# Transposing K of batches 2 and 3 in two steps of two head pairs, where there were four of one

## The chip, the cores and the metric

The kernel runs on one core of a Trainium2 chip. The metric is the device time of one execution in microseconds (us), taken as the median of several runs. A profile is one further execution with every engine recorded. Engines: TensorE (PE; its weight loads are PEld), VectorE (DVE), ScalarE (ACT), GpSimd (POOL) and SyncE (SP, which here only issues DMAs).

## The reference

Eight batches, 8 heads, 576 positions, head dimension 64. Attention with a decay bias and a causal mask, then RMS norm and a SwiGLU feed-forward network over all 4608 tokens:

```python
scores = (1 / sqrt(D)) * q @ k.T                        # per batch and head, 576 x 576
cum    = cumsum(maximum(s, 0)); bias = -(cum_i - cum_j)
scores = where(causal, -1e9, scores + minimum(bias, 0))
x      = softmax(scores) @ v                            # heads side by side: 4608 x 512
xn     = x / sqrt(mean(x * x) + 1e-6) * rms_g
out    = (silu(xn @ w_gate) * (xn @ w_val)) @ w_out     # 512 -> 1536 -> 512
```

Inputs and output are float32; the kernel multiplies in bfloat16.

## The kernel before

**Two kinds of work on one PE.** After batch 0, which is done by a prologue written out by hand, the feed-forward network runs in nine chunks of 512 tokens, and the attention of batches 1 to 7 is woven into it. `ffn(c)` (L658) is the frame. For each of 12 blocks `fb` of the hidden dimension it issues four gate matmuls (G, L668), a Tanh on ACT (L671), four value matmuls (V, L677) and on DVE the two products U (L680) and Ht (L673). Then come four output tiles of 12 matmuls (O, L690), each copied out by ACT (L695) and stored by SP (L697). G, V and O use four PSUM buffers in turn (`psF`): G of block `fb+2` takes the buffer of G of block `fb`, which is free once U of block `fb` has read it.

**The planner.** Between these groups `ffn` calls `step()` (L599), 36 times a chunk. One call is a *slot*. Chunk c has slots 36c+1 to 36c+36; 24 of them lie in the G/V part and 12 in the O part. The order that results is fixed when the program is built; every engine then runs its own instructions in that order and waits on semaphores. Slots are counted, not timed: the rules ask how many slots ago something was issued. In a slot `step()` does, in this order: what the last S step left pending; at most one `x_scale` (L335, DVE) with its `xt_dma` (L342, a DMA transpose on SP's queue); one item of ACT's side queue (loads of K and Q); one DMA transpose of Q or K (`kq_dma`, L171, on SP's queue); one item of the V loads and of POOL's casts; one check on DVE (L369, L375); and then PE work: an S step alone, or else an AV step and a T step if both are allowed.

The steps of attention, for batch b, with `g` for the two halves of the heads (head pairs 0 and 1, or 2 and 3):

- **T** (`t_step`, L180): K of one head pair is transposed by four PE matmuls against the identity into the bank `psT`, and one ACT copy (L192) spreads the 512 columns into `kqT`. `tail_step` (L194) does the same for the last 64 positions of all head pairs. In batches 2 and 3 K goes this way and Q goes through `kq_dma`; from batch 4 (`KB`) on there is no T at all. `psT` has one buffer, and AV with g = 1 uses it too (`psT32`).
- **S** (`s_step`, L225): scores of key block kb (0 to 4) and half g, then the exponentials on ACT (L274), half of them in the slot after, and the causal mask on POOL (L283). `psS` has one buffer.
- **AV** (`av_step`, L292): attention times V, a reciprocal and a product on DVE (L313, L315); with g = 1 also a sum of squares on ACT (L321) and its inverse root on POOL (L328, L331).
- **XT**: `x_scale` three slots after AV(b, qb, 1), and `xt_dma`, which puts 128 tokens into `xnT`. G of chunk c reads all 512 tokens of the chunk from there.

**What sets the order.** `t_seq`, `s_seq` and `av_seq` are consumed in order. `can_t` (L530) wants, for b of 2 or more:

```python
if b >= XB and at(*(("XT", 1, 3) if b == 2 else ("AV", b - 1, (2, 1, 0, 0, 0)[b - 3], 1))) > slot[0]:
    return False
if b >= XB and av_seq[0][2] == 1 and can_av(True):
    return False
if slot[0] - last["T"] < (1 if b < XB else 2 if b < 4 else 3) or slot[0] - last["AVT"] < 3:
    return False
```

So T of batch 3 may begin once AV(2, 2, 1) is done, two T steps are two slots apart, and a T step is three slots away from an AV step with g = 1 (`last["AVT"]`), in both directions. `can_s` (L540) wants the T steps of its two head pairs three slots back, the Q transposes five slots back, a free slot among eight E buffers, and a distance to the last S step that depends on a due time:

```python
due = SLOTS * ((b * S + kb * 128) // DM) - (26 if b == 1 else 18 if b < 4 else 14)
if slot[0] - last["S"] < (4 if slot[0] < due - 24 else 3 if slot[0] < due else 2):
```

`can_av` (L561) wants its S steps five slots back, two slots since the last AV, and XT of four row blocks earlier. `done["T", b, hp, w]`, written by `do_t` (L489), is where S looks for its transposes; `after_tail` queues the loads and casts of batch b + 2.

Of the kernel before, what the change touches and what calls it, by code (L numbers as in the profile page):

```python
# [12 lines left out]
AF = mybir.ActivationFunctionType  # L13
# [13 lines left out]
def kernel(  # L27
# [12 lines left out]
    nc = tc.nc  # L40
# [9 lines left out]
    HP = H // 2  # L50
# [7 lines left out]
    ident_bf = pers.tile([128, 128], BF16, name="ident_bf")  # L58
# [18 lines left out]
    kqn = mp.tile([128, 2, 2, NSC, H, D], BF16, name="kqn")  # L77
# [3 lines left out]
    kqTn = kqT.rearrange("d a w (h n) -> d a w h n", h=HP)  # L81
    kqTx = kqT.rearrange("d a w (c h n) -> d a w c h n", c=NSC, h=HP)
    XB = 2
    KB = 4
# [19 lines left out]
    def psF16():  # L104
        return pp.tile([128, 8, 128], BF16, name="psF16", tag="F", bufs=4)
# [10 lines left out]
    def psT():  # L116
        return pp.tile([128, 8, 128], BF16, name="psT", tag="T", bufs=1)
# [62 lines left out]
    def t_step(b, hp, w, pT=None, dve=None):  # L180
        pT = psT() if pT is None else pT
        dve = (w == 1) if dve is None else dve
        for r in range(4):
            nc.tensor.matmul(
                pT[:, r, :], lhsT=kqn[:, b % 2, w, r, 2 * hp:2 * hp + 2, :],
                rhs=ident_bf, is_transpose=True, start=(r == 0), stop=(r == 3))
        dst = kqTn[:, b % 2, w, hp, 0:512].rearrange("d (p r) -> d p r", r=4)
        src = pT[:, 0:4, :].rearrange("d r p -> d p r")
        if dve:
            nc.vector.tensor_copy(out=dst, in_=src)  # L190
        else:
            nc.scalar.activation(out=dst, in_=src, func=AF.Copy)  # L192

    def tail_step(b):  # L194
        pT = psT()
        nw = 2 if b < XB else 1
        for w in range(nw):
            for hp in range(HP):
                i = w * HP + hp
                nc.tensor.matmul(  # L200
                    pT[:, i, :], lhsT=kqn[:, b % 2, w, 4, 2 * hp:2 * hp + 2, :],
                    rhs=ident_bf, is_transpose=True, start=(i == 0), stop=(i == nw * HP - 1))
        dst, src = kqTn[:, b % 2, 0, :, 512:576], pT[:, 0:HP, 0:64]
        if b == 0:
            nc.vector.tensor_copy(out=dst, in_=src)
        else:
            nc.scalar.activation(out=dst, in_=src, func=AF.Copy)
        if nw == 2:
            nc.vector.tensor_copy(out=kqTn[:, b % 2, 1, :, 512:576], in_=pT[:, HP:8, 0:64])
# [163 lines left out]
    def check_max(i):  # L373
# [7 lines left out]
    slot = [0]  # L381
    first, chunk = [0], [0]
    done = {}
# [2 lines left out]
    s_seq.sort(key=lambda x: (1, 0, x[2], x[1]) if x[0] == 1 and x[1] < 2 else (x[0], x[1], x[2], 0))  # L386
    av_seq = [(b, qb, g) for b in range(B) for qb in range(NSC) for g in (0, 1)]
    xt_seq = [(b, qb) for b in range(B) for qb in range(NSC)]
    t_seq = [(b, hp, w) for b in range(KB) for hp in list(range(HP)) + ["tail"]
             for w in (0, 1) if w == 0 or (hp != "tail" and b < XB)]  # L390
    t_seq.sort(key=lambda x: (x[0], 9, 0, 0) if x[1] == "tail" else
               (x[0], x[1] // 2, x[2], x[1]) if x[0] == 1 else (x[0], x[2], x[1], 0))
# [86 lines left out]
    def after_tail(b):  # L479
        if b + 2 < B:  # L480
            casts(b + 2)
# [7 lines left out]
    def do_t(key, **kw):  # L489
        b, hp, w = key  # L490
        if hp == "tail":
            tail_step(b)
            done["T", b] = slot[0]
            after_tail(b)
        else:
            if b == 1:
                kw["dve"] = w == 1 and hp > 1
                if hp % 2:
                    kw["pT"] = psF16()
            t_step(b, hp, w, **kw)  # L500
        done["T", b, hp, w] = slot[0]
        last["T"] = slot[0]

    def do_s(key, pair=None):
# [94 lines left out]
    def step(bare=False):  # L599
# [31 lines left out]
        if can_s():  # L631
            pending.append(do_s(s_seq.pop(0)))
            if t_seq and t_seq[0][0] == 1 and can_t():
                do_t(t_seq.pop(0))
            return
# [7 lines left out]
        if n < 2 and t_seq and can_t():  # L643
            do_t(t_seq.pop(0))
# [126 lines left out]
    with tc.manual_schedule():  # L771
# [44 lines left out]
        load_v(0, 2)  # L816
        load_w(moe_w_gate, wg_sb, 0)
        do_t((0, 0, 0), pT=psT(), dve=False)
        do_t((0, 1, 0), pT=psF16(), dve=False)
        decay_sums()  # L820
# [65 lines left out]
        def done_cast(w):  # L886
# [11 lines left out]
                                        in_=moe_w_out.rearrange("(fc p) d -> p fc d", p=128)),  # L898
# [200 lines left out]
```

## Time and profile before

| | |
|---|---|
| median of 3 runs | 375.94 us (375.75 to 376.08) |
| the profiled execution | 375.92 us, span 374.2 us, 1.7 us outside it |
| PE busy | 347.0 us, 93% of the span |
| DVE, ACT, POOL busy | 279.7, 239.8, 174.4 us |
| T transposes (L184), all batches | 96 matmuls |
| ACT copies of T (L192) | 17, about 0.6 us each |
| granted TensorE clock | 0.998 of full |

The first G of chunk 1 starts 76.35 us into the span, of chunk 2 at 115.53 us, of chunk 3 at 155.60 us, of chunk 4 at 194.19 us. Busy shares are averages over the prologue, the woven stages and the last chunks, where no attention is left; stages have to be looked at one by one. A matmul's recorded duration is its passage through the pipeline (379 ns for one of 512 columns); what it takes from PE is the distance to the next start (a group of four: 0.86 us).

### The profile page before, as it was taken

What the parts mean: (1) busy time and instruction counts of PE and PEld (TensorE: products, weight loads), DVE (VectorE), ACT (ScalarE), POOL (GpSimd) and SP (SyncE); (2) the same over time, 40 slices, a digit from 0 to 9 for tenths busy, and PEclk for the clock granted to TensorE, in tenths of its full rate; (3) what the DMA queues carried; (4) which work ended last, traced back from release to release, by engine and by line L of the source; (5) the groups of instructions that cost most, each with busy time, mean ns of one, the idle gap of its engine ahead of it and who ended that gap; (6) DMA issues with size and microseconds to landing.
All of it is one profiled execution on the core that took longest, in us unless ns stands there. A gap on an engine that the chain in (4) does not pass through costs nothing. (4 is left out here: it accounts for less than half of the span.)

```text
span 374.2 us, 6937 instructions
## 1 busy us (share of the span) xinstructions
PE 347.0 (93%) x2356; PEld 161.4 (43%) x2356; DVE 279.7 (75%) x525; ACT 239.8 (64%) x626; POOL 174.4 (47%) x277
## 2 busy tenths in 40 slices
PE   1867899899999999899999999999999999999993
PEld 1443444454444444344444444444444444444441
DVE  6758988589887878788889897785488548837830
ACT  3777787547877597786777776777677744323321
POOL 5865734974846575779756825522322310000000
PEclk9999999999999999999999999999999999999999
DMA  8999999899997599959999997992210230020012
GB/s 230 189 227 237 146 196 220 123 204 225 155 168 105 53 195 165 159 55 204 149 162 225 136 107 152 120 67 44 96 26 14 44 105 3 0 84 31 0 44 76
DMA packets 125626, 46.22 MB, mean 124 GB/s; under 512 B 104912, under 2 KB 120784, under 8 KB 125584
## 3 DMA queue, kind: packets, MB, share of 16 engines
q0 software_dynamic: 59920, 11.80, 42.7%
q1 hardware_dynamic: 53040, 24.33, 34.6%
q10 hardware_dynamic: 12624, 9.59, 10.5%
q8 instruction: 20, 0.33, 0.4%
q14 instruction: 22, 0.18, 0.2%
HBM read 38.16 MB, written 9.44 MB: 127 GB/s over the span
## 5 line engine op out<-in xcount | busy, mean ns | idle before, releaser
L274 ACT ACTIVATE E<-psS,biasK 128x256 bf16<-128x256 f32 (+3 forms) x352 | 114.9, 415 | 19.7 <-PE psS L250 18.1
L668 PE MATMUL psF<-xnT,wg_sb 128*128 128x512 bf16 x432 | 111.1, 379 | 2.4 <-DMA xnT<-xs_sb 1.3
L677 PE MATMUL psF<-xnT,wv_sb 128*128 128x512 bf16 x432 | 111.1, 379 | 0.1
L690 PE MATMUL psF<-wout_sb,Ht 128*128 128x512 bf16 x432 | 102.3, 379 | 0.0
L283 POOL TENSOR_SCALAR_AFFINE_SELECT E<-E 128x512 bf16<-128x512 bf16 x72 | 52.2, 725 | 93.7 <-ACT E L274 92.8
L671 ACT ACTIVATE T<-psF 128x512 f32<-128x512 f32 x108 | 64.3, 597 | 42.1 <-PE psF L668 38.7
L680 DVE SCALAR_TENSOR_TENSOR U<-T,psF 128x512 bf16<-128x512 f32 x108 | 73.6, 682 | 21.9 <-ACT T L671 21.8
L673 DVE TENSOR_TENSOR Ht<-U,psF 128x512 bf16<-128x512 bf16 x99 | 67.7, 684 | 7.5 <-PE psS L250 0.5
L668 PEld LDWEIGHTS <-wg_sb 128*128 128x128 bf16 x432 | 38.7, 98 | 46.9 <-issue 8.0
L677 PEld LDWEIGHTS <-wv_sb 128*128 128x128 bf16 x432 | 38.6, 98 | 42.8 <-issue 4.6
L690 PEld LDWEIGHTS <-Ht 128*128 128x128 bf16 x432 | 38.7, 98 | 42.1 <-issue 2.3
L338 DVE SCALAR_TENSOR_TENSOR xs_sb<-x_sb,al_all,g_row 128x512 bf16<-128x512 bf16 (+1 forms) x40 | 32.8, 822 | 16.1 <-POOL al_all L331 14.5
L695 ACT ACTIVATE osb<-psF 128x512 f32<-128x512 f32 x36 | 21.4, 595 | 33.7 <-PE psF L690 29.4
L321 ACT ACTIVATE xs_sb<-x_sb 128x512 bf16<-128x512 bf16 (+1 forms) x36 | 22.9, 639 | 22.3 <-DVE x_sb L315 22.2
L175 POOL DMA_DIRECT2D v_sb<-in_v_dram x40 | 35.3, 883 | 0.4 <-issue 0.3
L375 DVE TENSOR_TENSOR acc<-acc,mag 128x1280 bf16<-128x1280 bf16 x32 | 29.4, 936 | 0.4
L250 PE MATMUL psS<-kqT 64*128 64x256 bf16 (+2 forms) x304 | 26.8, 262 | 1.6 <-ACT E L274 1.5
L306 PEld LDWEIGHTS <-E 128*128 128x128 bf16 x320 | 22.3, 99 | 13.3 <-POOL E L283 3.4
L328 POOL TENSOR_SCALAR al_all<-ss_all 128x1 f32<-128x1 f32 (+1 forms) x40 | 11.1, 277 | 28.5 <-ACT xs_sb L321 23.0
L300 PEld LDWEIGHTS <-E 128*128 128x128 bf16 x256 | 20.6, 99 | 7.9 <-DVE x_sb L315 0.6
L331 POOL TENSOR_TENSOR al_all<-al_all,mhalf 128x1 f32<-128x1 f32 (+1 forms) x40 | 22.2, 556 | 3.3
L250 PEld LDWEIGHTS <-kqT 64*128 64x128 bf16 x320 | 10.4, 97 | 29.9 <-issue 28.6
(94 smaller groups left out, 278.8 us busy)
## 6 DMA issues: line engine op xcount, KB each, us to landing
out_dram<-osb SPq DMA_DIRECT2D x36, 256.0 KB, 2.3
kq<-in_q_dram ACTq DMA_DIRECT2D x6, 1024.0 KB, 9.5
v_sb<-in_v_dram POOLq DMA_DIRECT2D x32, 128.0 KB, 7.2
kq<-in_k_dram ACTq DMA_DIRECT2D x2, 1024.0 KB, 10.6
kqn<-in_k_dram POOLq DMA_DIRECT2D x16, 128.0 KB, 5.6
wg_sb<-in_moe_w_gate_dram POOLq DMA_DIRECT2D x2, 768.0 KB, 7.3
wv_sb<-in_moe_w_val_dram POOLq DMA_DIRECT2D x2, 768.0 KB, 10.3
wout_sb<-in_moe_w_out_dram POOLq DMA_DIRECT2D x1, 1536.0 KB, 14.1
```

Of the source, the lines that this page charges most:

```text
L175: nc.gpsimd.dma_start(out=v_sb[0:n, b % 2, c, :, 0:64], in_=v[b, :, c * 128:c * 128 + n, :].rearrange("h p d -> p h d"))
L250: nc.tensor.matmul(pair[par][:, j * W:j * W + M], lhsT=kT, rhs=qT, start=(j == 0), stop=(j == nj - 1))
L274: nc.scalar.activation(out=eo, in_=ei, func=AF.Exp, scale=0.125, bias=biasK[:, kb, bh:bh + 1])
L283: nc.gpsimd.affine_select(out=Ev[:, :, 0:nq], in_=Ev[:, :, 0:nq], pattern=[[0, nh], [1, nq]], compare_op=ALU.is_ge, fill=0.0, base=0, chan ...
L338: nc.vector.scalar_tensor_tensor(out=xs_sb[0:n, (b * NSC + qb) % NX, :], in0=x_sb[0:n, (b * NSC + qb) % NX, :], scalar=al_all[0:n, col:col ...
L375: nc.vector.tensor_tensor(out=acc[:, sl], in0=acc[:, sl], in1=mag[:, sl], op=ALU.max)
L668: nc.tensor.matmul(Gp, lhsT=wg_sb[:, cc, fs], rhs=xnT[:, cc, x0:x0 + DM], start=(cc == 0), stop=(cc == CC - 1))
L671: nc.scalar.activation(out=T, in_=Gp, func=AF.Tanh, scale=0.5)
L673: nc.vector.tensor_tensor(out=Ht[:, fb - 1, :], in0=pend[0], in1=pend[1], op=ALU.mult)
L677: nc.tensor.matmul(Vp, lhsT=wv_sb[:, cc, fs], rhs=xnT[:, cc, x0:x0 + DM], start=(cc == 0), stop=(cc == CC - 1))
L680: nc.vector.scalar_tensor_tensor(out=U, in0=T, scalar=1.0, in1=Gp, op0=ALU.add, op1=ALU.mult)
L690: nc.tensor.matmul(Op, lhsT=Ht[:, fb, tb * 128:(tb + 1) * 128], rhs=wout_sb[:, fb, :], start=(fb == 0), stop=(fb == FB - 1))
```

## The change

For batches 2 and 3 (`b >= XB`; T steps exist only for b < 4) a T step takes two head pairs: eight transposes, which fill the whole bank `psT`, and then two copies on the same engine as before. `t_seq` lists head pairs 0 and 2 only, and `do_t` notes both head pairs as done in the step's slot. Batches 0 and 1 are unchanged, and so is `tail_step`.

```diff
     def t_step(b, hp, w, pT=None, dve=None):
...
-        for r in range(4):
+        nh = 1 if b < XB else 2
+        for i in range(4 * nh):
+            j, r = hp + i // 4, i % 4
             nc.tensor.matmul(
-                pT[:, r, :], lhsT=kqn[:, b % 2, w, r, 2 * hp:2 * hp + 2, :],
-                rhs=ident_bf, is_transpose=True, start=(r == 0), stop=(r == 3))
-        dst = kqTn[:, b % 2, w, hp, 0:512].rearrange("d (p r) -> d p r", r=4)
-        src = pT[:, 0:4, :].rearrange("d r p -> d p r")
-        if dve:
-            nc.vector.tensor_copy(out=dst, in_=src)
-        else:
-            nc.scalar.activation(out=dst, in_=src, func=AF.Copy)
+                pT[:, i, :], lhsT=kqn[:, b % 2, w, r, 2 * j:2 * j + 2, :],
+                rhs=ident_bf, is_transpose=True, start=(i == 0), stop=(i == 4 * nh - 1))
+        for i in range(nh):
+            dst = kqTn[:, b % 2, w, hp + i, 0:512].rearrange("d (p r) -> d p r", r=4)
+            src = pT[:, 4 * i:4 * i + 4, :].rearrange("d r p -> d p r")
+            if dve:
+                nc.vector.tensor_copy(out=dst, in_=src)
+            else:
+                nc.scalar.activation(out=dst, in_=src, func=AF.Copy)
...
-    t_seq = [(b, hp, w) for b in range(KB) for hp in list(range(HP)) + ["tail"]
+    t_seq = [(b, hp, w) for b in range(KB) for hp in list(range(0, HP, 1 if b < XB else 2)) + ["tail"]
              for w in (0, 1) if w == 0 or (hp != "tail" and b < XB)]
...
         done["T", b, hp, w] = slot[0]
+        if b >= XB and hp != "tail":
+            done["T", b, hp + 1, w] = slot[0]
         last["T"] = slot[0]
```

## The prediction

> **What bounds the kernel now.** I read the page's first part, then the waits of PE in the stage that the change touches, then the timeline there. The page:
>
> ```profile
> PE 347.0 (93%) x2356; PEld 161.4 (43%) x2356; DVE 279.7 (75%) x525; ACT 239.8 (64%) x626; POOL 174.4 (47%) x277
> ```
>
> PE is the bound, and what it idles is mostly prologue. The waits of PE between 76 and 156 us, chunks 1 and 2, which hold all T steps of batches 2 and 3 (line, what it waited for, us in total, times, longest):
>
> ```profile
> PE psF L668 <- DMA xnT<-xs_sb: 1.3, 1, 1.3
> PE psF L668 <- DVE U L680: 0.4, 1, 0.4
> PE psS L250 <- ACT E L274: 0.2, 1, 0.2
> ```
>
> Three places, under 2 us. A T step in the timeline (start, length, engine, line):
>
> ```profile
> 80.05 1.03 PE L668 MATMUL psF<-xnT,wg_sb 128*128 128x512 bf16 x4
> ...
> 80.91 0.39 PE L184 MATMUL psT<-ident_bf,kqn 128*128 128x128 bf16 x4
> ...
> 81.14 1.03 PE L677 MATMUL psF<-xnT,wv_sb 128*128 128x512 bf16 x4
> 81.17 0.60 ACT L671 ACTIVATE T<-psF 128x512 f32<-128x512 f32 x1 [0.67 <-PE psF L668]
> ...
> 81.67 0.59 ACT L192 ACTIVATE kqT<-psT 128x512 bf16<-128x512 bf16 x1
> ```
>
> Starts matter: G takes 80.91 - 80.05 = 0.86 us, four transposes 0.23 us, and V follows with no gap. A T step has no overhead on PE beside its transposes. The start of chunk 3:
>
> ```profile
> 151.24 1.21 SPq L348 DMA_TRANSPOSE xnT<-xs_sb  x1
> ...
> 153.91 0.39 PE L250 MATMUL psS<-kqT 64*128 64x256 bf16 x4
> ...
> 155.60 1.02 PE L668 MATMUL psF<-xnT,wg_sb 128*128 128x512 bf16 x4 [1.30 <-DMA xnT<-xs_sb]
> ```
>
> An S step takes 0.32 us (the one at 132.69 is followed by V at 133.01), so G was due at 154.23 and began 1.37 us late: the transpose of XT(3, 2), sent by SP at 151.24, had not landed.
>
> **The transposes and copies themselves: nothing.** Per batch four steps of four (4 x 0.223 us from the starts) become two of eight: 0.89 us of PE both times. Four copies of 0.60 us stay four; ACT, 64% busy, now has two in a row, 1.2 us. They issue no DMA. The PE's sum is unchanged, so anything gained or lost comes through the order. Its cover: behind the copies on ACT stand the next Tanh and the S step's exponentials. The first step's copies (batch 2) would begin where the row at 81.67 begins and end near 82.9; the second step's transposes come about 83.1, and the next Tanh after them. If that cover fails, the second step waits for `psT`: 0 to 0.15 us; I take +0.05.
>
> **The order, by stepping through the planner's rules.** Before, the rules give T of batch 2 in slots 41, 43, 45, 47 and its tail in 49; T of batch 3 in 67, 70, 77, 83 and tail in 85. In batch 3 two of these were held back because an AV step with g = 1 lay in between. After: batch 2 in 41 and 43, tail 45; S(2,0,0) in 44 instead of 46, S(2,0,1) 47 instead of 50, then S in 50, 53, 55, 57, 61, 65, 68 where it was 53, 55, 57, 59, 63, 66, 69. AV(2,2,1) comes in 62 instead of 64, which opens T of batch 3: slot 66 (beside AV(2,3,0)) and slot 69, before AV(2,3,1) is ready; tail in 75, ten slots earlier. So S(3,0,1) falls from slot 86 to 74, and the S steps of batch 3 stand three slots apart (71, 74, 77, 80, 83, 86, then 90, 94, 98) where four were crammed into 89, 91, 93, 95. AV(3,2,1) goes from 100 to 93, and XT(3,2) from 103 to 96. Batch 4 then runs 5 or 6 slots earlier than before (its V loads also finish before slot 96 instead of carrying over), batches 5 to 7 four. Loads and casts of batch 5, queued behind the tail of batch 3, stay where they were: their first item waits for the check of slot 100. On SP's queue XT(3,2) moves ahead of four Q and K transposes of batch 4; on POOL the inverse roots and masks come among casts (79 to 84) and V loads (from 85) instead of behind them.
>
> **What that is worth.**
>
> Chunk 3 starts at slot 109. With XT(3,2) seven slots earlier, at about 1.1 us a slot, 7.6 us lie against a lateness of 1.37: gone, -1.37.
>
> Two small waits in batch 2 go: the tail's transposes waited for the copy of step 47 (due 88.39 + 0.86 = 89.25, began 89.36), and a G waited for a late U (due 83.94, began 84.06): -0.22. What is late next there is V or G itself, at PE's rate.
>
> S steps that waited for the exponentials of the one before (`psS` has one buffer): an S step costs 0.10 us of gap by itself, and those at 134.90, 137.30 and 139.85 had 0.05, 0.11 and 0.15 more, the one at 101.36 had 0.23. At three or four slots of distance they go: -0.54.
>
> The wait of 0.4 us for U in chunk 1. The rows:
>
> ```profile
> 90.35 2.27 DVE L375 TENSOR_TENSOR acc<-acc,mag 128x1280 bf16<-128x1280 bf16 x1
> 90.39 1.17 POOL L149 CAST kqn<-kq 128x512 bf16<-128x512 f32 x2
> ...
> 92.54 0.67 DVE L680 SCALAR_TENSOR_TENSOR U<-T,psF 128x512 bf16<-128x512 f32 x1
> ...
> 93.27 1.02 PE L668 MATMUL psF<-xnT,wg_sb 128*128 128x512 bf16 x4 [0.38 <-DVE U L680]
> ```
>
> A check of 0.82 us (median of 32) took 2.27 beside POOL's casts; U came late, and G began 0.54 us after it was due (91.87 + 0.86). Check and casts keep their slots; AV(2,0,0), 0.60 us of DVE, moves into the check's slot, ahead of that U. Between the wait gone (-0.54) and all 0.60 us added I take +0.30, nearer the upper end, since what made it stands still. The Trainium skill (SBUF — State Buffer, "Who interferes with whom") says that a VectorE instruction with two SBUF inputs contends with a GpSimd one that reads SBUF, and that the first to issue blocks the other throughout; L375 beside a cast is that case and the trace agrees, 2.27 against 0.82 us. By the rule alone the stall recurs in full, and the sum below would be 374.7; were 0.82 us the rule, it would be 373.6.
>
> The end of G/V in chunk 2 gets denser on DVE. Slots 87 to 96: five U and five Ht (0.682 and 0.684 us), five AV (0.175 + 0.423), three x_scale (0.822): 12.3 us. PE in the same slots: ten groups of 0.863, two S of 0.43, five AV of 0.24: 10.7 us. DVE falls 1.6 us behind. G two blocks later needs U, so about one block (1.7 us) may be lost without a wait; and the first O tile reads the last Ht with its 12th matmul, which in the profile started near 143.91 (first at 141.30), while that Ht was done at 142.45: 1.46 us of margin. I take +0.30; from none to 3.8 (below).
>
> Batches 4 to 7: their waits (0.64, 0.30 and 0.20 us in the starts at 193.9, 212.1 and 179.1) may go (-1.1), or others of such size come (+0.6). I take 0.
>
> Sum: -1.37 - 0.22 - 0.54 + 0.30 + 0.30 + 0.05 = -1.48. The profiled execution took 375.92 us (span 374.2 and 1.7 around it, which nothing here touches), 0.02 from the median: 374.4.
>
> **Rivals.** *DVE becomes the bound at the end of chunk 2* (slower). Place: slots 87 to 96. An x_scale there can stretch to its longest (1.29 against 0.75 us) and wait for the inverse root as long as the longest in chunks 1 and 2 (0.7 us), with U and Ht queued behind it and PE behind those: three of them add 3.7 us to the lag of 1.6. Of these 5.3 us all beyond 1.46 is paid, 3.8 us instead of 0.30: 377.9. It turns the result from a lag of 3.2 us on. For it: DVE was busy 26.4 of the 28.45 us from 76.35 on, in chunk 1. Against: there, at the same load, it cost PE 0.65 us in all. [...] Chance 0.14.
>
> *The wait at chunk 3 stays* (no change): XT(3,2) is issued earlier by the planner, but SP sends in order, and five transposes of batch 4 took it 7.5 us from 130.84 on; x_scale itself may also be late. Then -1.37 is missing: 375.8. Against: 13 slots, some 14 us, remain to land it. Chance 0.12.
>
> *The later waits go too*: -1.1 more, 373.3. For it: S is one slot further apart there. Chance 0.13.
>
> That the change doesn't do what it says I leave out: bank, copies and `done` entries are plain in the diff.
>
> **Numbers.** The forecast, 374.4, has the remaining 0.61; by its unknowns alone it lies between 373.7 and 375.1. The range reaches to the other cases, 373.1 to 377.0, leaving out most of the slow rival's upper half and a little below. About 0.2% (0.75 us) is what a measurement of this kernel can tell from no change. Faster than that: forecast and third rival, less a little, 0.73; same: the second, 0.13; slower 0.14.
>
> **What would show it.** In the profile after: no DMA among PE's waits after 100 us; T steps of 0.45 us, two per batch, the last two before chunk 2 begins; L192 still 17 times 0.6 us; no S to S distance of two slots in chunk 2; PE without idle around the first O tile of chunk 2. A DVE wait of PE over 1 us there, or the DMA wait still at a chunk's start, would make the forecast wrong.

## The result: 0.8% slower, and the profile after

The changed kernel took 379.04 us in the median of six runs, 376.01 for the kernel before beside it: a ratio of 1.0077, 95% interval 1.0063 to 1.009. The forecast was 374.4 us. The profiled execution took 378.57 us, span 377.4 us; its mean granted clock was 0.987, but five other executions with 0.996 to 0.999 took 378.8 to 379.1 us, so the clock is not the cause.

The slots are those that the prediction derived, for each T, S and AV step of batches 2 and 3. The merged step itself runs as forecast, too. Its timeline, in the changed kernel (lines have moved by 3 to 6: G is L674, V L683, U L686, Ht L679, O L696, S L254, exponentials L278, sums of squares L325, AV's product L319, x_scale L342, checks L373 and L379):

```profile
80.88 0.61 PE L187 MATMUL psT<-ident_bf,kqn 128*128 128x128 bf16 x8
...
81.33 1.03 PE L683 MATMUL psF<-xnT,wv_sb 128*128 128x512 bf16 x4
...
81.63 1.08 ACT L196 ACTIVATE kqT<-psT 128x512 bf16<-128x512 bf16 x2
...
83.05 0.61 PE L187 MATMUL psT<-ident_bf,kqn 128*128 128x128 bf16 x8
```

Eight transposes take 0.45 us from start to start, the two copies are done at 82.7, and the second step follows its G (82.19 + 0.86) without a wait. The waits of PE over 76 to 200 us, the same columns as before (line, what it waited for, us in total, times, longest); the first line is the kernel before, whose waits for the DMA and for U in this longer window are those shown above (1.3 and 0.4 us):

```profile
PE psS L250 <- ACT E L274: 0.7, 2, 0.6
```

and the kernel after:

```profile
PE psS L254 <- ACT E L278: 5.0, 5, 1.5
PE psF L674 <- DVE U L686: 0.4, 1, 0.4
PE psF L683 <- DVE Ht L679: 0.3, 1, 0.3
```

The DMA wait of 1.3 us is gone, as forecast. In its place five S steps wait, 5.0 us together, for ACT to finish the exponentials of the S step before, which hold the only `psS`. From the starts of the PE groups between 76 and 215 us, everything over its usual length adds up to 6.7 us (3.9 before); the first matmul of the verdict (L756, the kernel's closing test of its ranges, after all attention) begins 2.8 us later. So, within what two single executions can tell, the whole loss is in these waits. The longest of them, and how it came about, DVE first:

```profile
90.33 2.12 DVE L379 TENSOR_TENSOR acc<-acc,mag 128x1280 bf16<-128x1280 bf16 x1
92.37 0.17 DVE L317 RECIPROCAL rZ<-psAV 128x4 f32<-128x4 f32 x1
92.57 0.42 DVE L319 TENSOR_TENSOR x_sb<-psAV,rZ 128x256 bf16<-128x256 f32 x1
92.91 0.68 DVE L686 SCALAR_TENSOR_TENSOR U<-T,psF 128x512 bf16<-128x512 f32 x1
...
95.11 0.42 DVE L319 TENSOR_TENSOR x_sb<-psT,rZ 128x256 bf16<-128x256 f32 x1
```

then ACT and the S step on PE:

```profile
95.57 0.63 ACT L325 ACTIVATE xs_sb<-x_sb 128x512 bf16<-128x512 bf16 x1 [1.99 <-DVE x_sb L319]
96.10 0.19 ACT L325 ACTIVATION_READ_ACCUMULATOR xs_sb<-x_sb 128x1 f32 x1
96.19 0.58 ACT L677 ACTIVATE T<-psF 128x512 f32<-128x512 f32 x1
96.67 1.56 ACT L278 ACTIVATE E<-psS,biasK 128x256 bf16<-128x256 f32 x4
...
98.28 0.39 PE L254 MATMUL psS<-kqT 64*128 64x256 bf16 x4 [1.45 <-ACT E L278]
```

Read it from the top. In slot 49 a check that takes 0.82 us elsewhere took 2.12 us beside POOL's casts, and AV(2,0,0), now in the same slot, stands behind it. The check is 1.3 us longer than usual and the two instructions of that AV step add 0.6, so the next U is almost 2 us late, and the product of AV(2,0,1), slot 52, ends at 95.5. The sum of squares of that step is in ACT's queue ahead of everything that came later. ACT idles 1.99 us in front of it, with the exponentials of S(2,1,1), slot 53, queued behind although their scores were done at 95.0; then the sum of squares and a Tanh take 1.1 us more, and the exponentials start at 96.67. S(2,2,0), slot 55, needs that `psS`, and PE stands for 1.45 us. It is a chain through four queues: DVE late, ACT's head of line, `psS`, PE.

### The profile page after: what moved, and what is told of

The parts are those of the page before. It is cut to its first block, busy times and chain, and to the rows that moved or that the text cites. A ratio compares the mean times of both kernels' runs of the same rounds, so it can differ in the third digit from the quotient of the medians.

```text
span 377.4 us, 6953 instructions
## 1 busy us (share of the span) xinstructions
PE 346.5 (92%) x2356; PEld 161.1 (43%) x2356; DVE 282.1 (75%) x525; ACT 239.4 (63%) x626; POOL 172.5 (46%) x277
## 4 chain that ended last, share of the span: by engine, by line
PE 46%; DVE 6%; POOL 4%; issue 3%; ACT 2%; POOLq 0%; DVEq 0%; ACTq 0%
PE psF L683 14%; PE psF L674 14%; PE psF L696 14%; PE psS L254 2%; DVE acc L379 1%; POOL v_sb L175 1%; DVE mag L373 1%; POOL kqn L155 1%; DVE Ht L679 1%; DVE x_sb L319 1%; POOL al_all L335 1%; ACT E L278 1%; DVE xs_sb L342 1%; DVE U L686 1%; POOL E L287 1%
## 5 line engine op out<-in xcount | busy, mean ns | idle before, releaser
L278 ACT ACTIVATE E<-psS,biasK 128x256 bf16<-128x256 f32 (+3 forms) x352 | 116.4, 415 | 19.9 <-PE psS L254 17.5
L674 PE MATMUL psF<-xnT,wg_sb 128*128 128x512 bf16 x432 | 111.2, 380 | 1.2 <-ACT xnT L368 0.7
L683 PE MATMUL psF<-xnT,wv_sb 128*128 128x512 bf16 x432 | 111.0, 379 | 0.5 <-DVE Ht L679 0.5
L696 PE MATMUL psF<-wout_sb,Ht 128*128 128x512 bf16 x432 | 101.9, 380 | 0.0
L686 DVE SCALAR_TENSOR_TENSOR U<-T,psF 128x512 bf16<-128x512 f32 x108 | 73.7, 682 | 22.9 <-ACT T L677 22.9
L679 DVE TENSOR_TENSOR Ht<-U,psF 128x512 bf16<-128x512 bf16 x99 | 67.8, 685 | 8.7 <-PE psS L254 1.0
L674 PEld LDWEIGHTS <-wg_sb 128*128 128x128 bf16 x432 | 38.7, 98 | 46.8 <-issue 7.0
L696 PEld LDWEIGHTS <-Ht 128*128 128x128 bf16 x432 | 38.8, 98 | 43.3 <-issue 3.1
L683 PEld LDWEIGHTS <-wv_sb 128*128 128x128 bf16 x432 | 38.7, 98 | 42.1 <-issue 3.5
L342 DVE SCALAR_TENSOR_TENSOR xs_sb<-x_sb,al_all,g_row 128x512 bf16<-128x512 bf16 (+1 forms) x40 | 34.0, 853 | 14.9 <-POOL al_all L335 13.1
L325 ACT ACTIVATE xs_sb<-x_sb 128x512 bf16<-128x512 bf16 (+1 forms) x36 | 22.9, 640 | 30.2 <-DVE x_sb L319 30.1
L254 PE MATMUL psS<-kqT 64*128 64x256 bf16 (+2 forms) x304 | 26.6, 261 | 5.8 <-ACT E L278 5.8
L379 DVE TENSOR_TENSOR acc<-acc,mag 128x1280 bf16<-128x1280 bf16 x32 | 29.1, 935 | 0.2
L254 PEld LDWEIGHTS <-kqT 64*128 64x128 bf16 x320 | 10.4, 97 | 34.3 <-issue 33.8
L332 POOL TENSOR_SCALAR al_all<-ss_all 128x1 f32<-128x1 f32 (+1 forms) x40 | 9.6, 239 | 32.4 <-ACT xs_sb L325 26.4
```

The lines of the kernel that those rows point to most:

```text
L254: nc.tensor.matmul(pair[par][:, j * W:j * W + M], lhsT=kT, rhs=qT, start=(j == 0), stop=(j == nj - 1))
L278: nc.scalar.activation(out=eo, in_=ei, func=AF.Exp, scale=0.125, bias=biasK[:, kb, bh:bh + 1])
L342: nc.vector.scalar_tensor_tensor(out=xs_sb[0:n, (b * NSC + qb) % NX, :], in0=x_sb[0:n, (b * NSC + qb) % NX, :], scalar=al_all[0:n, col:col ...
L379: nc.vector.tensor_tensor(out=acc[:, sl], in0=acc[:, sl], in1=mag[:, sl], op=ALU.max)
L674: nc.tensor.matmul(Gp, lhsT=wg_sb[:, cc, fs], rhs=xnT[:, cc, x0:x0 + DM], start=(cc == 0), stop=(cc == CC - 1))
L679: nc.vector.tensor_tensor(out=Ht[:, fb - 1, :], in0=pend[0], in1=pend[1], op=ALU.mult)
```

## Experiments

Three theories. *A, later D:* the merge costs nothing; the new order puts an AV step with g = 1 in the slot ahead of an S step where DVE is late, and DVE's lateness reaches PE through the sum of squares, the exponentials and `psS`. *M:* the merged step itself costs, by two copies in a row. *L:* ACT is simply outrun by S steps three slots apart.

### 1. The merge alone, in the old order

```diff
+        if b >= XB:
+            return slot[0] == AT[b, hp]      # 43, 47, 49; 70, 83, 85
...
+        if slot[0] in (41, 45, 67, 77):
+            last["T"] = slot[0]
```

> The merged T steps, but every S, AV and XT step in the slot it had before the change (merged T in slots 43 and 47, 70 and 83; tails 49 and 85). Theory A (the loss is the order: an AV step with g = 1 now stands in the slot ahead of S steps, its sum of squares on ACT waits for DVE, and the exponentials behind it keep psS): the time is that of before, 375.5 to 376.5 us, and the PE waits for psS stay near the 0.2 us that the profile of before has between 76 and 156 us. Rival M (the merge itself costs: two copies in a row on ACT, the bank held longer): 377.5 to 379 us, with waits at the merged steps.

Measured: 376.18 us, ratio 0.9998 (0.9974 to 1.0021). The first lines of PE's waits (76 to 200 us) are back to

```profile
PE psF L680 <- DMA xnT<-xs_sb: 1.8, 2, 1.4
PE psT L204 <- ACT kqT L196: 0.2, 1, 0.2
PE psS L254 <- ACT E L278: 0.2, 1, 0.2
```

M falls: half the steps with twice the work cost nothing that can be told (the interval is 0.9 us to either side). The second line is the tail step of batch 2, which waits for the two copies: its transposes begin 0.4 us late here, 0.1 before. The change's effect of 3 us is its order.

### 2. The sums of squares on DVE in five places

```diff
-        act = act or b > 1 or b == 1 and qb > 1
+        act = (act or b > 1 or b == 1 and qb > 1) and (b, qb) not in (
+            (2, 0), (2, 2), (3, 2), (3, 4), (4, 4))
```

> The changed kernel, with the sums of squares of five AV steps (batch and row block 2,0; 2,2; 3,2; 3,4; 4,4) on DVE instead of ACT; these are the ones behind which exponentials queued in the five places where PE waited for psS, 5.0 us together. Theory A: these waits go, DVE has 5 x 0.78 us more, of which perhaps 1 us is felt: 374.5 to 375.5 us. Rival L (ACT simply has too much work there, so that S steps three slots apart outrun it): each place gains at most the 0.83 us of ACT work taken away, 4.1 us in the best case but less in the three that waited 0.9 us or under, and ACT shows no idle ahead of the squares: 376.0 to 377.5 us.

Measured: 381.19 us, ratio 1.0145 (1.0102 to 1.0188), a miss for both theories in the time. PE's waits, 76 to 200 us:

```profile
PE psF L674 <- DVE U L686: 2.2, 2, 1.8
PE psT L310 <- POOL E L287: 1.6, 1, 1.6
PE psF L683 <- DVE Ht L679: 0.6, 1, 0.6
PE psS L254 <- ACT E L278: 0.5, 2, 0.3
```

The waits for `psS` fell from 5.0 to 0.5 us, so the sums of squares were indeed what the exponentials stood behind. But PE now waits for U, for Ht and for a mask on POOL. ACT was the road, not the source: with DVE late, the lateness reaches PE without ACT, too. That turned theory A into D, in which the source is DVE. This run alone does not show it, because the edit also adds work to DVE: each square takes 0.77 us there, and an x_scale at 98.98 took 3.75 us beside POOL, where the changed kernel has 2.60. Experiments 5 to 7 test it.

### 3 and 4. One batch alone

```diff
-        nh = 1 if b < XB else 2
+        nh = 2 if b == 2 else 1              # 3 for the other kernel
```

(and the same condition in `t_seq` and `do_t`)

> Only batch 2's T steps are merged; batch 3 keeps four. The planner then puts S and AV of batch 2 where the changed kernel has them (to slot 68), and from slot 88 on within one slot of the order of before. Theory A: it pays the waits of the slots 52, 55 and 68 (about 0.1 + 1.5 + 0.9 us against before) and keeps the late start of chunk 3 (XT(3,2) in slot 102, one slot earlier than before): 377.5 to 378.7 us. Rival M: half of the loss, 377.3 to 377.8 us.

> Only batch 3's T steps are merged. Batch 2 keeps its order of before; XT(3,2) comes in slot 97 instead of 103 and batch 4 about five slots earlier. Theory A: no wait at slots 52 to 68, the 1.3 us wait at chunk 3 gone, and of the later waits for psS in the changed kernel (slots 98, 109 and 143, 2.7 us) those that keep the same neighbours stay: 374.5 to 377 us. Rival M: half of the loss, 377.3 to 377.8 us.

Measured: batch 2 alone 378.59 us, ratio 1.007 (1.0043 to 1.0097). That is the time expected, but made up otherwise: the late start of chunk 3 shrank to 0.4 us, and three S steps near 137, 140 and 142 us waited 0.6, 0.5 and 0.4 us, which theory A did not have. Batch 3 alone 381.18 us, ratio 1.0142 (1.0121 to 1.0164): worse than both together, which neither theory had. Each order meets its own collisions; they don't add. Its worst new one (DVE, then POOL, then part of PE's waits for 76 to 200 us):

```profile
127.67 3.34 DVE L342 SCALAR_TENSOR_TENSOR xs_sb<-x_sb,al_all,g_row 64x512 bf16<-64x512 bf16 x1 [0.20 <-POOL al_all L335]
130.94 0.17 DVE L317 RECIPROCAL rZ<-psAV 128x4 f32<-128x4 f32 x1
```

```profile
127.60 1.16 POOL L149 CAST kqn<-kq 128x512 bf16<-128x512 f32 x2
128.72 0.63 POOL L287 TENSOR_SCALAR_AFFINE_SELECT E<-E 128x512 bf16<-128x512 bf16 x1
129.31 0.60 POOL L149 CAST kqn<-kq 128x512 bf16<-128x512 f32 x1
129.87 0.60 POOL L141 CAST kqn<-kq 128x512 bf16<-128x512 f32 x1
```

```profile
PE psF L683 <- DVE Ht L679: 1.6, 1, 1.6
```

An x_scale that takes 0.75 us in the median stood 3.34 us while POOL ran five instructions in a row.

### 5 and 6. Both orders without the checks

```diff
-            lambda w=w: check_mag(b, w), lambda: check_max(0), lambda: check_max(1),
+            lambda w=w: b < 1 and check_mag(b, w), lambda: b < 1 and check_max(0), ...
```

> The changed kernel without the range checks on DVE for batches 1 to 7 (leaves out L373 and L379 there, some 40 us of DVE work; every other instruction keeps its slot). Theory D (the new order puts AV steps with g = 1 and S steps where DVE is behind with checks, some of them stretched beside POOL's casts; DVE's lateness goes through the sum of squares on ACT to the exponentials, to psS, to PE): four of the five waits for psS go (98.3, 113.9, 159.4 and 196.6 us, 4.9 us together), and the G at 93.6 (0.5); the kernel lands at 373 to 374.5 us and is no slower than the kernel before without checks. Rival L (ACT is outrun by S steps three slots apart, whatever DVE does): the waits for psS stay above 3 us and the time above 377.

> The kernel before, without the same checks (the other half of the pair). Theory D: little to gain, the 0.5 us at 93.3 and 0.6 us at 193.9; the 1.4 us at the start of chunk 3 stays: 374.5 to 375.3 us. With the other half this says whether the order of the changed kernel is worse in itself or only through the checks. Rival L: same time for this one, 2 to 3 us under its partner.

Measured: the new order 374.53 us, ratio 0.9968 (0.9953 to 0.9982); the old one 374.78 us, ratio 0.9973 (0.9959 to 0.9988). The first is at the upper end of what was expected, the second within it. With DVE relieved, 3 us of difference become none that can be told. The new order's waits for `psS` (76 to 200 us) fall to 1.1 us, and the old one's late chunk start shrinks only by half; their first lines:

```profile
PE psS L254 <- ACT E L278: 1.1, 2, 0.6
```

```profile
PE psF L668 <- DMA xnT<-xs_sb: 0.7, 1, 0.7
PE psS L250 <- ACT E L274: 0.6, 3, 0.2
```

L falls for the most part: S steps at three slots' distance are no burden for ACT when DVE is on time; what is left to it, at most, is that 1.1 us. Most of it is the S step of the chain above, which stands two slots behind the one before it: of its 1.52 us, 0.71 stay even without the checks, where the sum of squares and the Tanh still stand ahead of the exponentials. The new order is not measurably worse in itself, but it needs DVE where DVE is full.

### 7. One check moved

```diff
-                return slot[0] % 2 and chunk[0] == b
+                return (slot[0] % 2 or slot[0] >= 44) and chunk[0] == b
```

> The changed kernel; only the three DVE instructions of the check of batch 1's K move, from slots 45, 47, 49 to 44, 45, 46, out of the reach of POOL's casts that begin in slot 47. Theory D: the 2.1 us instruction at 90.3 becomes 0.82, and with it the two waits that follow it go (0.49 at 93.6 and 1.52 at 98.3): 376.7 to 377.5 us. If those waits come from the S steps' spacing, nothing changes: 379.

Measured: 376.99 us, 2.05 under the changed kernel, ratio to before 1.003 (1.0018 to 1.0042). The G at 93.6 no longer waits; of the 1.52 us at 98.3, 0.71 stay. The check is back to its usual length and ACT stands less before the sum of squares:

```profile
88.38 0.82 DVE L379 TENSOR_TENSOR acc<-acc,mag 128x1280 bf16<-128x1280 bf16 x1
```

```profile
94.59 0.63 ACT L325 ACTIVATE xs_sb<-x_sb 128x512 bf16<-128x512 bf16 x1 [0.58 <-DVE x_sb L319]
```

The time is the one expected, but by luck in part: 0.49 us went at the G and 0.81 at 98.3, and 0.86 more at the S step that had waited 0.98 us at 113.9, which had not been tied to this check; how it hangs on it is not shown. Three DVE instructions moved by one to three slots, PE's order untouched, make up about three fifths of the loss (ratio 1.003 where it was 1.0077).

### 8 and 9. The checks behind AV, and both moves

```diff
-        run_side(dve_side)                   # ahead of S, AV and T
...
+        run_side(dve_side)                   # at the end of the slot
```

> The changed kernel with each check issued at the end of its slot, behind the AV step's two DVE instructions and not ahead of them. Theory D: the AV step of slots 62, 105 and 139 comes 0.8 us or more earlier on DVE, so the waits at 113.9, 159.4 and 196.6 (0.98, 0.96, 1.43) fall to some 0.2, 0.2 and 0.6; the pair at 93.6 and 98.3 gets shorter by about 0.3 at most, as the check there still stands ahead of U: 376 to 377.3 us. Rival L: 378.5 to 379.5.

> The changed kernel with both moves of the checks, batch 1's K check early and every check behind the AV work of its slot. Theory D, if the places were independent: 2.0 us less from the first move, the three waits of the output parts shorter by 1.9 from the second, and the 1.2 us that the second move brought elsewhere (a late Ht at 211) back again: about 376.3 us, 375.5 to 377.2. If later lateness grows whenever something earlier shrinks, it stays at 377 or above.

Measured: 379.61 us for the first (ratio 1.0106, 1.0076 to 1.0136), no gain and a miss. The three waits that follow the checks of the output parts did fall, 0.98 to 0.12, 0.96 to 0.43, 1.43 to 0.91; but later ones grew, a V that waited 0.36 us for Ht near 211 us now waits 1.57. There x_scale stood 2.28 us for the inverse root from POOL, with Ht behind it. Both moves together gave a median of 378.64 us, ratio 1.0074 (1.0042 to 1.0106), a miss too. Three of the ten runs took 376.2 to 376.4 us, where they were expected, the other seven 378.5 to 381.8. The profiled one took 376.32 us, with 4.7 us of waits instead of 6.7, as if the places were independent; why other executions of the same program take up to 5.5 us longer no profile here shows, and it stays open.

### 10. A version under both

The kernel before, with the early check and one Q transpose put behind XT(3,2) on SP's queue (the K transpose that follows it moves two slots, too):

```diff
-                return slot[0] % 2 and chunk[0] == b
+                return (slot[0] % 2 or slot[0] >= 44) and chunk[0] == b
...
-        if not moved and x_seq and slot[0] - last["X"] >= 2:
+        if not moved and x_seq and slot[0] - last["X"] >= 2 and slot[0] != 102:
```

> The kernel before (four single T steps) with two moves: batch 1's K check in slots 44 to 46, and the Q transpose of slot 102 put off, so that SP sends XT(3,2) of slot 103 ahead of it and the last two transposes of batch 4 two slots later. Theory D and the late start of chunk 3: the 0.54 us at 93.3 goes, and 0.8 of the 1.37 us at 155.6 (SP could send XT from 150.4 on, when x_scale ends, instead of 151.24): 374.4 to 375.2 us, under both kernels. If DVE's stretched check and the order on SP's queue don't matter: 375.9.

Measured: 375.32 us, ratio 0.9978 (0.9961 to 0.9994), a little faster than before and just above what was expected. The late G at 93.3 is gone. XT(3,2) went out at 149.93, 1.3 us earlier. But it took 4.7 us to land instead of 4.3, and its G was itself due 0.5 us earlier, since the wait at 93.3 is gone; so the delay of that G fell only from 1.37 to 1.04 us, where 0.6 was expected. The second row is the other half of XT(3,2), for the next chunk:

```profile
149.93 1.17 SPq L348 DMA_TRANSPOSE xnT<-xs_sb  x1
151.15 1.25 SPq L350 DMA_TRANSPOSE xnT<-xs_sb  x1
```

```profile
154.75 0.59 PE L668 MATMUL psF<-xnT,wg_sb 128*128 128x512 bf16 x2 [0.97 <-DMA xnT<-xs_sb]
```

### 11. The stretched x_scale moved out of the casts

In the kernel of experiment 4:

```diff
-            if ready(3, "AV", b, qb, 1):
+            if ready(3, "AV", b, qb, 1) and ((b, qb) != (2, 4) or slot[0] >= 85):
```

> The kernel with batch 3 alone merged (381.2 us), with one DVE instruction moved: x_scale(2,4) from slot 82, where it ran beside POOL's casts of slots 79 to 83 and took 3.34 us, to slot 85, behind them. Theory D with the casts as what stretches it: it takes about 0.75 us there, the PE wait of 1.6 us at 132.2 goes, and the time falls to 379.3 to 380.0 us. If the 3.34 us came from anything else (its own operands, the load on DVE), it stays long in slot 85 and the time at 381.

Measured: 379.70 us, ratio to before 1.0125 (1.0094 to 1.0156), 1.5 under experiment 4. The same instruction three slots later:

```profile
130.47 0.74 DVE L342 SCALAR_TENSOR_TENSOR xs_sb<-x_sb,al_all,g_row 64x512 bf16<-64x512 bf16 x1
```

The wait of 1.6 us at 132.2 is gone. What stretched it was POOL's work beside it.

## Why the prediction was wrong

By its own steps:

- *Transposes and copies: nothing.* Right, and shown by experiment 1. The second step did not wait for `psT` (0 in place of 0.05).
- *The order.* Right.
- *Chunk 3, -1.37, and the two waits of batch 2, -0.22.* Right: no DMA wait of PE after 76 us, no gap at the tail of batch 2.
- *S steps that waited for exponentials, -0.54.* This step failed, by the most. It took the distance between S steps as what decides the wait, and the exponentials as starting when the scores are done. In the profile after, five S steps wait 1.52, 0.98, 0.47, 0.96 and 1.43 us, 5.4 in place of the 0.54 of the old order that was to go and the 0.64 at 193.9. The first two, 2.50 us, are new waits that this term put at nothing; the others fall to the last two terms below. What was overlooked is what stands on ACT between the scores and the exponentials: the sum of squares of the AV step one slot earlier, which needs DVE. Experiment 2 shows that link; 5 and 7 show that DVE's checks feed it with about half of the longest wait, 0.81 of 1.52 us.
- *The late U in chunk 1, +0.30.* The stall recurred (0.49 against 0.54 us), near the no-change value. But the prediction ended its price at G. The same lateness went on through AV(2,0,1) to S(2,2,0), which waited 1.52 us; with the check moved (experiment 7) the first wait goes and 0.81 us of the second.
- *The dense end of chunk 2, +0.30.* No U or Ht was late for PE there; S(3,4,0) in slot 98 waited 0.47 us for exponentials. About right in size, by luck: the mechanism was another.
- *Batches 4 to 7, 0.* This step failed, too. Their waits came to 3.2 us (0.96 at 159.4, 0.46 at 174.4, 1.43 at 196.6, 0.36 at 211.5) against 1.1 before. The bound that was given, +0.6, was too small, since only waits that the old order showed had been priced.
- *The slower rival* named the right engine, a full DVE whose lateness is paid by PE, and the point that AV, checks and POOL meet there. It had the wrong place, slots 87 to 96, and the wrong road, U and Ht; the lateness came in where checks run every slot or casts run beside, and through ACT.

With what each term measured, the sum is 0 - 1.37 - 0.22 - 0.54 + 2.50 - 0.05 + 0.47 + 2.07 = +2.9 us, against the 2.8 of the two profiles and the forecast -1.48. The two failed steps bring 4.6 us of waits that the forecast had at nothing. Nearly all the signs named for a right forecast came true (no DMA wait, short T steps, no S steps two slots apart in chunk 2, no long DVE wait at its end), because they watched the places where the old order had waited.

The rule that the prediction weighed comes from the Trainium skill, SBUF — State Buffer, "Who interferes with whom": VectorE with two SBUF inputs contends with GpSimd's reads, and the loser is blocked for a whole instruction. The traces agree on who meets whom (2.12 us to 0.82 by moving the check, 3.34 to 0.74 by moving the x_scale). They go further on how long: the x_scale of 3.34 us ran beside five POOL instructions, so it was not let in after the first. Who came first cannot be read off the recorded starts to a hundredth: in the kernel before, the check began 0.04 us ahead of the first cast (90.35 and 90.39) and was still the one held.

## What to carry to other kernels

When an edit only changes an order, follow each newly adjacent pair through every in-order queue it shares, not only the two ends: here an AV step and an S step meet on ACT, and the first one's need of DVE becomes the second one's delay. A wait that recurs is not priced by its first victim; carry the lateness on until some slack takes it up. And before moving work towards an engine that is 75% busy on average, look at what that engine does in just those slots: with the checks gone, the order that had lost 3 us lost nothing that could be told.

## What the hardware showed that was not expected

- A VectorE x_scale of 0.75 us can be held beside several POOL instructions in a row: it took 2.60 us beside three casts and two masks, 3.34 us beside four casts and a mask, and 3.75 us beside seven such instructions (experiment 2). It need not wait for the last of them: the one of 2.60 us ended at 100.80, while POOL's masks and casts went on without a break to 102.40.
- Running beside POOL is not enough for that. In the changed kernel x_scale at 141.84 took its 0.75 us beside a mask that began 0.16 us after it, and there the mask was the longer one: 1.08 us instead of 0.64 in the median.
- The DMA transpose of XT(3,2) took 4.3 us from sending to landing in the kernel before and 4.7 us in experiment 10, which sent it 1.3 us earlier; what made it longer is not shown.
- Eight transposes into one bank cost PE the same 56 ns each as four, and two copies out of it 0.6 us each, as one.
